# A spectral filter and a gated feed-forward on one core: the excursions of transform stage A moved off stage B, a third input buffer, an output buffer moved to a lasting pool, and the last copies moved to VectorE

## The chip, the cores and the metric

The kernel runs on one core of one Trainium2 chip. Times are device microseconds (us). A profiled run also leaves a trace of every instruction and DMA, with a span a little shorter than the timed run (925.2 us for 927.0). In its lines PE is TensorE, PEld its weight loads, DVE VectorE, ACT ScalarE, POOL GpSimd and SP SyncE; a q behind the name is the engine's queue of instructions, which also issues DMAs. The DMA share is the mean busy share of 16 DMA engines as the profile reports it, and it reads over 1 in places (1.31 from 68 to 70 us).

## The reference

```python
def _attn_ref(x, filt_r, filt_i):                  # x: (8, 3008, 256)
    X = np.fft.rfft(x, axis=1)                     # along the 3008 positions
    Y = X * (filt_r + 1j * filt_i)[None, :, :]     # filters: (1505, 256)
    return np.fft.irfft(Y, n=x.shape[1], axis=1)

def _moe_ref(x, w_gate, w_val, w_out):             # 24064 tokens, 256 -> 1536 -> 256
    gate = np.maximum(x @ w_gate, 0.0)
    val = x @ w_val
    return (gate * val) @ w_out
```

## The kernel before

The Fourier transform is done as matmuls. For each of 8 batches, stage A transforms along 94 positions and goes through DRAM (Abuf), stage B transforms along the other 32, multiplies by the filter, transforms back, and goes through DRAM (Dbuf), and stage C finishes the inverse and leaves yT, the input of the feed-forward. The feed-forward runs over 47 blocks of 512 tokens, 12 steps each, 564 steps in all. The work of the stages for later batches is laid into these steps, so that TensorE never has to run it alone.

From batch 2 on, stage A is "tiled". A chunk of x is loaded (`load_chunk`), GpSimd folds it with sums and differences (`fold_chunk`), and TensorE does 16 small fp32 products on 24 x 32 tiles of the array into four PSUM banks (`tiled_a`). The trace has 32 matmul records for them. I call this an excursion; each batch has four.

```python
pro = prologue.enter_context(tc.tile_pool(name="pro", bufs=1))      # closed before the main loop
...
def items_a(b):                                   # stage A of batches 0 and 1, in the prologue
    def one(c, j, st):
        if j == 0:
            st["asb"] = pro.tile([NROW, NC2 * D], BF16, tag="asb", bufs=4, name="asb")
        ...                                       # matmul into psA
        nc.scalar.copy(dst, psA[0:NROW])
        if j == 3:
            nc.sync.dma_start(..Abuf[b].., st["asb"])
...
def load_chunk(b, j):
    xp = XP[j % 2]                                # two chunk buffers
    ...                                           # 4 + 2 DMAs from SP, about 0.9 MB
def fold_chunk(b, j):
    t = fs.tile([128, 2, 512], FP32, tag="fold", bufs=2, name="fold")
    ...                                           # six tensor_tensor on GpSimd
def tiled_a(b, j):
    banks = [ps.tile([128, 2, D], FP32, tag=t, name="psF") for t in ("psv", "psg", "fft", "fft")]
    ...                                           # 16 matmuls, 4 copies to asf, 4 DMAs to Abuf
...
def gv(blk, ft, prods):                           # one step of the feed-forward
    ...                                           # 4 matmuls of 512 columns: psV, psG
    vsb = fs.tile([128, W], BF16, tag="vsb", bufs=3)
    nc.scalar.copy(vsb, psV[:, :W])
    nc.vector.scalar_tensor_tensor(prod, in0=psG[:, :W], scalar=0.0, in1=vsb, op0=ALU.max, op1=ALU.mult)
...
prologue.close()
fs = ctx.enter_context(tc.tile_pool(name="fs", bufs=2))   # takes over the prologue's memory
...
    end = (b * S // W - 1) * NFT + C_AT[0] - 5
    sb0 = 19 if b == 1 else end - 30 | 1          # first step of stage B of batch b
    ...
        for j in range(4):
            e = sb0 - 16 - NFT * (3 - j)          # excursions at sb0 -52, -40, -28, -16
            at_step(e - 23, lambda b=b, j=j: load_chunk(b, j))
            at_step(e - 22, lambda b=b, j=j: fold_chunk(b, j))
            at_step(e, lambda b=b, j=j: tiled_a(b, j))
    for i, f in enumerate(items_b(b)):
        at_step(sb0 + 2 * i, f)                   # stage B on steps sb0 to sb0 + 26
    at_step(sb0 + 27, lambda b=b: load_d(b))      # dC <- Dbuf, for stage C
```

## Time and profile before

| | before |
|---|---|
| time, median of 3 runs | 926.65 us (926.38 to 926.66) |
| span of the profiled run | 925.2 us |
| start of the first main-loop step | 61.2 us |
| last step's start to the end | 12.6 us |
| TensorE busy | 897.4 us |

The shortest way in is the chain of work that ended last, followed back from the end: its shares of the span by engine.

```profile
PE 90%; DMA 4%; ACT 2%; DVE 2%; issue 1%; SPq 0%; POOL 0%; ACTq 0%; POOLq 0%
```

TensorE (PE) carries 90% of it. What is not PE there is time in which TensorE, the engine that sets the pace, waits for someone else, and that is where a change of schedule can gain. A "step" in this text runs from its first load of a value weight (WvT) to the next step's; the steps' lengths are read off the trace.

### The profile page before, as it was taken

What the parts mean: (1) busy time and instruction counts of PE and PEld (TensorE: products, weight loads), DVE (VectorE), ACT (ScalarE), POOL (GpSimd) and SP (SyncE); (2) the same over time, 40 slices, a digit from 0 to 9 for tenths busy, and PEclk for the clock granted to TensorE, in tenths of its full rate; (3) what the DMA queues carried; (4) which work ended last, traced back from release to release, by engine and by line L of the source; (5) the groups of instructions that cost most, each with busy time, mean ns of one, the idle gap of its engine ahead of it and who ended that gap; (6) DMA issues with size and microseconds to landing.
All of it is one profiled execution on the core that took longest, in us unless ns stands there. A gap on an engine that the chain in (4) does not pass through costs nothing.

```text
span 925.2 us, 17992 instructions
## 1 busy us (share of the span) xinstructions
PE 897.4 (97%) x6488; PEld 546.7 (59%) x6602; DVE 576.8 (62%) x871; ACT 505.3 (55%) x897; POOL 260.6 (28%) x180
## 2 busy tenths in 40 slices
PE   8779999999999999999999999999999999999997
PEld 3435665566655665556655566655665566666665
DVE  3716865568655686557755577555875568655552
ACT  4655555555555555555555555555555555555553
POOL 4320444404444054322543125440444400000000
PEclk9899999999999999999999999999999999999999
DMA  9996345353453533553344533535335252231111
GB/s 253 257 249 131 104 129 146 89 128 104 126 150 88 128 104 116 155 118 86 108 146 137 114 105 111 153 100 124 99 120 170 64 118 64 63 102 36 35 30 50
DMA packets 106138, 109.04 MB, mean 118 GB/s; under 512 B 9794, under 2 KB 87362, under 8 KB 105410
## 3 DMA queue, kind: packets, MB, share of 16 engines
q1 hardware_dynamic: 101222, 103.77, 40.4%
q0 software_dynamic: 4512, 3.90, 2.7%
q8 instruction: 52, 0.85, 0.4%
q14 instruction: 36, 0.29, 0.1%
q10 hardware_dynamic: 316, 0.22, 0.1%
HBM read 61.94 MB, written 49.81 MB: 121 GB/s over the span
## 4 chain that ended last, share of the span: by engine, by line
PE 90%; DMA 4%; ACT 2%; DVE 2%; issue 1%; SPq 0%; POOL 0%; ACTq 0%; POOLq 0%
PE psG L444 26%; PE psO L463 25%; PE psV L444 24%; PE psF L321 4%; PE psA L275 3%; PE psD L383 2%; PE psD L382 2%; PE psX L363 2%; PE psY L428 2%; DVE prod L449 2%; ACT vsb L447 1%; DMA XF<-in_x_dram 1%; DMA Dbuf<-dsb 1%; DMA Abuf<-asb 1%; DMA out_dram<-osb 1%
## 5 line engine op out<-in xcount | busy, mean ns | idle before, releaser
L449 DVE SCALAR_TENSOR_TENSOR prod<-psG,vsb 128x512 bf16<-128x512 f32 x564 | 389.9, 692 | 288.5 <-ACT vsb L447 277.8
L447 ACT CAST vsb<-psV 128x512 bf16<-128x512 f32 x564 | 331.5, 588 | 270.2 <-PE psV L444 159.4
L463 PE MATMUL psO<-WoT,prod 128*128 128x256 bf16 x2256 | 336.6, 273 | 1.3
L444 PE MATMUL psG<-yT,WgT 128*128 128x512 bf16 x1102 | 331.1, 380 | 4.0
L444 PE MATMUL psV<-yT,WvT 128*128 128x512 bf16 x1041 | 318.7, 381 | 6.8 <-ACT vsb L447 4.5
L463 PEld LDWEIGHTS <-prod 128*128 128x128 bf16 x2256 | 220.6, 98 | 143.5
L444 PEld LDWEIGHTS <-WgT 128*128 128x128 bf16 x1128 | 110.3, 98 | 134.8 <-issue 2.2
L307 POOL TENSOR_TENSOR fold<-XP 128x1024 f32<-128x1024 f32 x24 | 56.4, 2348 | 416.0 <-DMA out_dram<-osb 151.4
L444 PEld LDWEIGHTS <-WvT 128*128 128x128 bf16 x1128 | 102.5, 98 | 38.5 <-issue 26.8
L385 ACT CAST dsb<-psD 128x512 bf16<-128x512 f32 x96 | 55.9, 587 | 51.8 <-PE psD L383 50.1
L468 ACT COPY osb<-psO 128x512 f32<-128x512 f32 (+1 forms) x96 | 55.3, 577 | 31.9 <-PE psO L463 24.5
L366 DVE TENSOR_TENSOR tt<-psX,Ftr 128x512 bf16<-128x512 f32 x96 | 65.2, 681 | 4.3 <-PE psX L363 4.3
L372 DVE TENSOR_TENSOR uu<-psX,Fti 128x512 bf16<-128x512 f32 x90 | 61.3, 681 | 0.0
L308 POOL TENSOR_TENSOR XP<-XP 128x1024 f32<-128x1024 f32 x24 | 56.4, 2350 | 1.9
L383 PE MATMUL psD<-uu,I2u 128*128 128x256 bf16 x192 | 47.7, 276 | 0.6 <-POOL uu L370 0.6
L382 PE MATMUL psD<-tt,I2t 128*128 128x256 bf16 x192 | 47.9, 276 | 0.0
L327 DVE CAST asf<-psF 128x512 bf16<-128x512 f32 x48 | 31.5, 687 | 16.6 <-PE psF L321 15.9
L363 PE MATMUL psX<-at,F 128*128 128x256 bf16 x192 | 37.8, 281 | 4.1 <-DMA at<-Abuf 4.1
L433 ACT CAST yT<-psY 128x512 bf16<-128x512 f32 x47 | 27.5, 585 | 24.0 <-PE psY L428 23.9
L435 DVE CAST yT<-psY 128x512 bf16<-128x512 f32 x47 | 32.0, 681 | 12.9 <-PE psY L428 12.9
L428 PE MATMUL psY<-M,dC 96*128 96x94 bf16 (+18 forms) x604 | 37.7, 199 | 1.1 <-DMA dC<-Dbuf 1.1
L321 PE MATMUL psF<-XP,WF 24*32 24x512 f32 x384 | 37.1, 597 | 0.0
(63 smaller groups left out, 437.9 us busy)
## 6 DMA issues: line engine op xcount, KB each, us to landing
dC<-Dbuf SPq DMA_DIRECT2D x64, 192.0 KB
XP<-in_x_dram SPq DMA_DIRECT2D x48, 256.0 KB
Dbuf<-dsb SPq DMA_DIRECT2D x31, 384.0 KB
XP<-in_x_dram SPq DMA_DIRECT2D x96, 96.0 KB
Abuf<-asf SPq DMA_DIRECT2D x96, 96.0 KB
at<-Abuf SPq DMA_DIRECT2D x48, 192.0 KB
out_dram<-osb SPq DMA_DIRECT2D x70, 94.0 KB
XF<-in_x_dram SPq DMA_DIRECT2D x12, 256.0 KB
```

The lines of the kernel that those rows point to most:

```text
L307: tt(t, xp[:, 0:2], xp[:, 2:4], op=ALU.add)
L308: tt(xp[:, 2:4], xp[:, 0:2], xp[:, 2:4], op=ALU.subtract)
L321: nc.tensor.matmul(banks[q][32 * c:32 * c + 32], WF[r:r + 24, c, :], fold[b, j][c][r:r + 24], start=True, stop=True, tile_position=(r, 32 ...
L363: nc.tensor.matmul(psX[:, i], F2[:, g + i, :], at[:, g + i, :], start=True, stop=True)
L366: nc.vector.tensor_tensor(tt, psX, Ftr[:, g:g + 2, :], op=ALU.mult)
L372: nc.vector.tensor_tensor(uu, psX, Fti[:, g:g + 2, :], op=ALU.mult)
L382: nc.tensor.matmul(psD[:, i], I2t[:, g + i, :], tt[:, i], start=True, stop=False)
L383: nc.tensor.matmul(psD[:, i], I2u[:, g + i, :], uu[:, i], start=False, stop=True)
L444: nc.tensor.matmul(pt[:, :W], w[:, h, ft * 128:(ft + 1) * 128], yt[:, h, :], start=(h == 0), stop=(h == 1))
L447: nc.scalar.copy(vsb, psV[:, :W])
L449: nc.vector.scalar_tensor_tensor(prod, in0=psG[:, :W], scalar=0.0, in1=vsb, op0=ALU.max, op1=ALU.mult)
L463: nc.tensor.matmul(psO[:, t % 2], prods[ft][:, t * 128:(t + 1) * 128], WoT[:, ft, :], start=(ft == 0), stop=(ft == NFT - 1))
```

## The change

Its intent is to let each excursion run in a step that has nothing but feed-forward work, to give x chunks the buffer that this spacing needs, to keep the output buffer of stage A out of the memory that the main loop takes over, and to free ScalarE at the end.

```diff
@@ items_a
-                st["asb"] = pro.tile([NROW, NC2 * D], BF16, tag="asb", bufs=4, name="asb")
+                st["asb"] = sb.tile([128, NC2 * D], BF16, tag="asb", bufs=4, name="asb")
@@ load_chunk, fold_chunk
-        xp = XP[j % 2]
+        xp = XP[(4 * b + j) % 3]
@@ tiled_a
-        asf = fs.tile([128, 2, 4, D], BF16, tag="asf", bufs=2, name="asf")
+        asf = sb.tile([128, NC2 * D], BF16, tag="asb", bufs=4, name="asb")
+        asf = asf.rearrange("p (n q d) -> p n q d", n=2, d=D)
@@ o_part
-            nc.scalar.copy(osb[:, t0 % 2:t % 2 + 1], psO[:, t0 % 2:t % 2 + 1])
+            copy = nc.vector.tensor_copy if last else nc.scalar.copy
+            copy(osb[:, t0 % 2:t % 2 + 1], psO[:, t0 % 2:t % 2 + 1])
@@ clear_chunks
-        for i in range(2):
+        for i in range(3):
@@ the schedule
-            for j in range(4):
-                e = sb0 - 16 - NFT * (3 - j)
-                at_step(e - 23, lambda b=b, j=j: load_chunk(b, j))
-                at_step(e - 22, lambda b=b, j=j: fold_chunk(b, j))
-                at_step(e, lambda b=b, j=j: tiled_a(b, j))
-            at_step(e + 4, lambda b=b: load_at_tiled(b))
+            for j, (l, e) in enumerate(((-66, -41), (-60, -33), (-54, -27), (-40, -17))):
+                at_step(sb0 + l, lambda b=b, j=j: load_chunk(b, j))
+                at_step(sb0 + l + 1, lambda b=b, j=j: fold_chunk(b, j))
+                at_step(sb0 + e, lambda b=b, j=j: tiled_a(b, j))
+            at_step(sb0 + e + 4, lambda b=b: load_at_tiled(b))
```

The slices that fit the larger buffer are left out. Line numbers shift by one or two: L444 (gv) is L445 after, L447 (vsb) L448, L468 (osb) L470, L476 (stores) L478, L428 (stage C) L429.

More of the change, by code (lines that the diff above doesn't have):

```diff
@@ L276, in one @@
                              start=True, stop=True)
-            dst = st["asb"][:, j * 512:(j + 1) * 512]
+            dst = st["asb"][:NROW, j * 512:(j + 1) * 512]
             nc.scalar.copy(dst, psA[0:NROW])
@@ L280, in one @@
                 nc.sync.dma_start(_ap(Abuf[b], c * NROW * NC2 * D, [[NC2 * D, NROW], [1, NC2 * D]]),
-                                  st["asb"])
+                                  st["asb"][:NROW])
         for c in range(N2 // NC2):
@@ L302, in fold_chunk @@
     def fold_chunk(b, j):
-        xp = XP[j % 2]
+        xp = XP[(4 * b + j) % 3]
         t = fs.tile([128, 2, 512], FP32, tag="fold", bufs=2, name="fold")
```

## The prediction

> **What bounds the kernel now.** I read the page's busy table first, then TensorE's waits, then the timeline around each place where TensorE is late, and last the clock in those stretches. In the page a line of the table is engine, busy us, share of the span, instructions:
>
> ```profile
> PE 897.4 (97%) x6488; PEld 546.7 (59%) x6602; DVE 576.8 (62%) x871; ACT 505.3 (55%) x897; POOL 260.6 (28%) x180
> ```
>
> TensorE is the bound: VectorE and ScalarE rest over a third of the span. 97% cannot be taken at its word, since a matmul is shown with its pipeline time (0.38 us for one whose successor starts 0.21 us later), so small gaps hide in it. I therefore measured steps. The main loop has 564 steps (47 blocks of 12), and I call a step the time from its first load of value weights to the next step's. 345 steps that do only feed-forward work have a median of 1.300 us (eight matmuls of 512 or 256 columns); 64 steps with a full share of stage B 1.955; 18 steps with one tiled A excursion 2.757; 6 with both, 4.288. Only what makes a step longer than its matmuls need can be won, so I looked for those. TensorE's waits (us in total, times, longest):
>
> ```profile
> PE psV L444 <- ACT vsb L447: 4.5, 1, 4.5
> PE psX L363 <- DMA at<-Abuf: 4.1, 1, 4.1
> ...
> PE psY L428 <- DMA dC<-Dbuf: 1.1, 1, 1.1
> ```
>
> The first stands at the start of the main loop. The view of the tile asb (A's output buffer) says whom it holds up:
>
> ```profile
> L280 SPq DMA_DIRECT2D Abuf<-asb x8: 303/309/437, 12.4 to 61.5; - x8
> ...
> POOL XP L562: 10.5, 1
> ACT vsb L447: 5.8, 1
> ```
>
> The last write of asb to DRAM is issued at 61.5; the first vsb copy, which reads only PSUM, waits for it, because vsb lies in memory that the closing prologue pool gives up and asb is in that pool. The completion counts put its landing at 67.33. The stretches (us, then busy us of PE, PEld, DVE, ACT, POOL; granted clock; DMA share; GB/s) show the second half of the price:
>
> ```profile
> 62.00:64.00 2.00, 1.83 (x7) 0.78 (x8) 0.07 (x1) 0.00 (x0) 0.00 (x0) 1.00 1.09 310
> 64.00:68.00 4.00, 0.00 (x0) 0.00 (x0) 0.00 (x0) 0.22 (x1) 0.31 (x1) 0.75 1.22 274
> 68.00:70.00 2.00, 1.58 (x4) 0.56 (x4) 1.29 (x2) 1.39 (x3) 2.00 (x2) 0.50 1.31 215
> 70.00:72.00 2.00, 2.00 (x6) 0.76 (x5) 0.69 (x1) 0.64 (x2) 1.24 (x1) 0.50 1.30 215
> 72.00:74.00 2.00, 2.00 (x8) 0.79 (x7) 1.19 (x2) 0.80 (x2) 0.00 (x0) 0.80 1.17 325
> ```
>
> No matmul for 4 us, then half clock until about 73. The other place is the excursion that falls on a stage B step. From the timeline (start, us, engine, line, instruction, count, idle before and who ended it), one such excursion, then one on a free step:
>
> ```profile
> 127.14 0.61 PE L321 MATMUL psF<-XP,WF 24*32 24x512 f32 x1
> ...
> 127.88 0.10 PEld L321 LDWEIGHTS psF<-XP,WF 24*32 24x32 f32 x1 [0.57 <-ACT dsb L385]
> ...
> 128.28 0.10 PEld L321 LDWEIGHTS psF<-XP,WF 24*32 24x32 f32 x1 [0.24 <-DVE uu L372]
> ...
> 129.50 0.38 PE L444 MATMUL psV<-yT,WvT 128*128 128x512 bf16 x1 [0.16 <-issue]
> ```
>
> ```profile
> 146.37 0.61 PE L321 MATMUL psF<-XP,WF 24*32 24x512 f32 x1
> ...
> 147.63 0.61 PE L444 MATMUL psV<-yT,WvT 128*128 128x512 bf16 x2
> ```
>
> 2.36 us against 1.26 for the same 32 matmuls: of the four PSUM banks that an excursion needs, two are the pair tagged "fft", which stage B's dsb copy and uu product still hold.
>
> [...] Here the last asb write, issued from SP, took 5.8 us (61.5 to 67.3), at a DMA share over 1. [...]
>
> **The change part by part.** (1) asb in the lasting pool. The built program agrees: the first vsb copy no longer waits for any asb write, only for things done by 61 (x loads, the small "last" read, the last A matmul). Saved: step 2 takes 6.114 us against 0.862 for its neighbour, 5.25; steps 3 and 4, at the low clock, 1.707 and 1.577, 0.85 and 0.71 too much. Sum **6.8 us**, all on TensorE's path. The wait for yT before step 0 (0.69 in the timeline) stays.
>
> (2) Excursions moved. With a batch's stage B on steps 0 to 26 after sb0 and a period of 72, the first of each batch's four sat at -52, which is +20 of the batch before. The new places, -41, -33, -27, -17, are +31 and later: all free, and none shares a step with stage C. Batches 2 to 7 have one bad one each: 6 x ((4.288 - 1.955) - (2.757 - 1.300)) = 6 x 0.876 = **5.3 us**. The step after is 1.207 in both kinds, so nothing is paid later. The other 18 move from one free step to another: 0. They leave step 5 of a block, where the output copy uses ScalarE, for 4, 0 and 6; adding up the copies (0.59 and 0.69 us each) after an excursion at step 4, every bank is free before TensorE wants it.
>
> (3) A third chunk buffer: 1.8 us more memset on GpSimd (3.54 for two) near 61 to 67, beside everything; the first chunk load is at step 27 now. It allows the close spacing. The fold tile keeps two buffers, so the third fold waits for the first excursion: six operations, 2 x 2.35 + 4 x 1.27 = 9.8 us, due 14 steps later (14 x 1.30 + 1.36 = 19.6). Hidden.
>
> (4) Last copies on VectorE. The last matmul ends at 919.4 (913.58 + 5.84), the last copy starts at 921.73, because ScalarE also issues stores, and its issues wait:
>
> ```profile
> 917.49 2.87 ACTq L476 DMA_DIRECT2D out_dram<-osb  x3
> 920.47 0.37 ACT L468 COPY osb<-psO 128x256 f32<-128x256 f32 x1 [3.01 <-DMA out_dram<-osb]
> ...
> 921.73 0.37 ACT L468 COPY osb<-psO 128x256 f32<-128x256 f32 x1 [0.89 <-ACT osb L468]
> ```
>
> The copies will come 2 us earlier, but three issues in 2.87 us against two in 0.70 shows that the stores wait for the landing of stores before them, on a semaphore used again. That stays. I choose **0.5 us** of the 2.3.
>
> Sum: 6.8 + 5.3 + 0.5 = 12.6; 926.65 - 12.6 = **914.1 us**, 1.4% less.
>
> **The rivals.** First, a new wait takes the old one's place. The loop start comes 6.8 us earlier for loads whose issue does not move. Landing in this trace and new need: second half of gate weights 65.3, step 6 at 67.6; third dC part 69.3, step 8's stage C at 69.8; second half of output weights 73.4, about 76. The middle one has 0.5 us; a DMA share over 1 speaks for trouble, the unchanged queue order against it. It would cost 0.5 to 2 us, more if the clock drops again. Second, the dC wait: one stage C start out of six waited (1.1 us near 483), another had only about 0.3 us to spare. The x loads around it move; the two outcomes, no wait and two or three, are -1 to +2 us. Third, excursions at the new places find their own bank or copy waits; 24 x 0.2 would be 5 us and take back part 2. Against it: the 18 free ones agree within 0.15 us. Fourth, the end is bound by stores and part 4 is nil: +0.5; or the semaphores clear early: -1.5.
>
> **Range and chances.** All parts right and the dC wait gone gives 912; part 4 nil with two new waits of 1.5 us gives 917.5. I take 911.8 to 917.6. Faster by over 2% needs below 908.1, which is 6 us beyond every gain I can find: 2%. Slower by 2% needs 19 us of new waiting: 1%.
>
> **What would show it.** TensorE's waits no longer name vsb; clock 1.00 through 62 to 76; the first main-loop steps all near 0.86; no step above 2.8 us among those with an excursion; idle before weight loads in excursions ended by nothing of stage B; last output copies on VectorE within 1 us of their matmuls, and the end about 4 to 5 us after the last matmul. It is wrong if psY waits for dC near 70, if the excursions at the new steps exceed 2.757, or if a fold of GpSimd ends a wait of TensorE.

## The result, and the profile after

The changed kernel took 913.28 us (913.1 to 913.37, 4 runs) against 926.65 in the same rounds (926.38 to 926.96). A ratio in this document is the mean time of one kernel's runs over that of the other's runs of the same rounds, so it is not quite the ratio of the medians. Here it is 0.9855 (95% interval 0.9838 to 0.9872), 13.4 us less.

The chain of the changed kernel shows the gain in one line: what was DMA, ACT, DVE and "issue" has become PE.

```profile
PE 95%; DMA 3%; SPq 0%; ACT 0%; POOL 0%; DVE 0%; issue 0%; ACTq 0%; POOLq 0%
```

TensorE's waits after the change (us in total, times, longest) no longer name vsb in the first place, nor psY waiting for dC at all. What is left are the start-up waits and sub-microsecond ones (the longest four):

```profile
PE psX L364 <- DMA at<-Abuf: 3.9, 1, 3.9
PE psJ L489 <- DVE junk L495: 2.5, 1, 2.5
PE psA L275 <- DMA XF<-in_x_dram: 1.7, 2, 1.5
PE psV L445 <- ACT yT L434: 0.7, 1, 0.7
```

The same stretches at the start of the main loop (us, busy us of PE, PEld, DVE, ACT, POOL, then granted clock, DMA share, GB/s): TensorE is busy and the clock stays at 1.00, while the DMA columns are almost those of before.

```profile
64.00:68.00 4.00, 4.00 (x21) 1.82 (x19) 3.30 (x5) 2.63 (x5) 2.16 (x2) 1.00 1.21 281
68.00:70.00 2.00, 2.00 (x16) 1.06 (x15) 1.55 (x3) 1.45 (x3) 0.00 (x0) 1.00 1.31 214
70.00:72.00 2.00, 2.00 (x17) 1.01 (x15) 1.38 (x2) 1.69 (x4) 0.00 (x0) 1.00 1.30 217
```

The first excursion of batch 2 in the timeline, now on a free step: first product at 135.90, next feed-forward matmul at 137.16, that is 1.26 us where the kernel before needed 2.36.

```profile
135.90 0.61 PE L321 MATMUL psF<-XP,WF 24*32 24x512 f32 x1
...
137.16 0.60 PE L445 MATMUL psV<-yT,WvT 128*128 128x512 bf16 x2
```

Where the 13.96 us between the two profiled spans come from:

| stretch | before, us | after, us | difference |
|---|---|---|---|
| to the first step's start | 61.16 | 61.03 | -0.12 |
| steps 0 to 11 | 18.29 | 11.48 | -6.81 |
| steps 12 to 562 | 833.16 | 826.40 | -6.77 |
| last step's start to the end | 12.63 | 12.37 | -0.26 |

The third row splits further. The six excursions on stage B steps gave 6 x 0.876 = 5.26. Step 272 had been 2.848 us against a median of 1.609 for its kind, because stage C waited for dC: 1.24. The remaining 0.27 is mostly a handful of excursions a little under the median of 2.757.

### The profile page after: what moved, and what is told of

It reads as the page before. It is cut to its first block, busy times and chain, and to the rows that moved or that the text cites. A ratio compares the mean times of both kernels' runs of the same rounds, so it can differ in the third digit from the quotient of the medians.

```text
span 911.3 us, 18044 instructions
## 1 busy us (share of the span) xinstructions
PE 896.0 (98%) x6602; PEld 545.7 (60%) x6602; DVE 578.0 (63%) x875; ACT 500.8 (55%) x893; POOL 262.4 (29%) x181
## 4 chain that ended last, share of the span: by engine, by line
PE 95%; DMA 3%; SPq 0%; ACT 0%; POOL 0%; DVE 0%; issue 0%; ACTq 0%; POOLq 0%
PE psV L445 27%; PE psG L445 27%; PE psO L464 26%; PE psF L321 3%; PE psA L275 3%; PE psY L429 2%; PE psD L383 2%; PE psD L384 2%; PE psX L364 2%; DMA XF<-in_x_dram 1%; DMA Abuf<-asb 1%; DMA at<-Abuf 0%; DMA out_dram<-osb 0%; SPq L178 0%; SPq L478 0%
## 5 line engine op out<-in xcount | busy, mean ns | idle before, releaser
L448 ACT CAST vsb<-psV 128x512 bf16<-128x512 f32 x564 | 332.0, 589 | 244.7 <-PE psV L445 206.4
L445 PE MATMUL psV<-yT,WvT 128*128 128x512 bf16 x1128 | 335.9, 379 | 0.9 <-ACT yT L434 0.7
L445 PE MATMUL psG<-yT,WgT 128*128 128x512 bf16 x1128 | 335.3, 379 | 0.0
L445 PEld LDWEIGHTS <-WgT 128*128 128x128 bf16 x1128 | 110.0, 98 | 133.8 <-issue 0.5
L445 PEld LDWEIGHTS <-WvT 128*128 128x128 bf16 x1128 | 102.3, 98 | 33.1 <-issue 20.9
L470 ACT COPY osb<-psO 128x512 f32<-128x512 f32 x92 | 53.9, 586 | 22.7 <-PE psO L464 20.3
L328 ACT CAST asb<-psF 128x512 bf16<-128x512 f32 x48 | 25.8, 589 | 32.5 <-PE psF L321 32.5
L328 DVE CAST asb<-psF 128x512 bf16<-128x512 f32 x48 | 30.9, 686 | 17.3 <-PE psF L321 14.5
L429 PE MATMUL psY<-M,dC 96*128 96x94 bf16 (+18 forms) x604 | 37.5, 198 | 0.0
```

What stands on the lines that cost most here:

```text
L328: copy(asf[:, :, q, :], banks[q])
L445: nc.tensor.matmul(pt[:, :W], w[:, h, ft * 128:(ft + 1) * 128], yt[:, h, :], start=(h == 0), stop=(h == 1))
```

## The experiments

Twelve runs were made, all correct. The first three are parts of the change taken alone.

**Only the buffer** (e1_pool).

```diff
 # from the kernel before
-                st["asb"] = pro.tile([NROW, NC2 * D], BF16, tag="asb", bufs=4, name="asb")
+                st["asb"] = sb.tile([NROW, NC2 * D], BF16, tag="asb", bufs=4, name="asb")
```

> The kernel before with only A's output buffers of the prologue moved to the lasting pool. Theory (the wait of the first vsb copy on the last A store, plus the half clock after it): 6.8 us less than before, about 919.8 us; steps 2, 3 and 4 of the main loop at 0.86 us, clock 1.00 from 62 to 76. Rival (another load takes the wait's place): 1 to 5 us less, with a new TensorE wait near 65 to 76. The excursions on stage B steps stay at 4.29 us, and the wait for dC near 480 may stay or move.

Measured: 919.70 us against 926.70, ratio 0.9928 (0.9915 to 0.9941), 6.7 us less. Steps 2, 3 and 4 take 0.863, 0.864 and 0.863 us, steps 0 to 11 together 11.48 (the changed kernel: 11.48), the six excursions on stage B steps still 4.288. The theory holds, and no later load took over the wait, so the rival is out. Stage C did not wait for dC in this profile, although no load was moved; I come back to this below.

**Only the steps and the third buffer** (e2_steps): the schedule, `XP` and `clear_chunks` parts of the diff above, applied to the kernel before.

> The kernel before with only the excursions moved and the third chunk buffer. Theory: 5.3 us from the six bad excursions, and 1.2 us from the wait for dC, which I now take to be an effect of where the x chunks are loaded and not of chance: 6.5 us less in all, about 920.2 us; all 24 steps with an excursion at 2.65 to 2.9 us, the first dC part landing 2 to 4 us ahead of its use for every batch (before: -1.4 to 2.3 us). Rival (the dC wait was chance): 5.3 us less, and the room before dC's use as in the kernel before. The stall at step 2 stays at 6.1 us.

Measured: 920.59 us, ratio 0.9936 (0.9924 to 0.9947), 5.9 us less. In its profile steps 12 to 562 take 826.68 us, 6.5 less than before, as worked out. Its first step began 1.0 us later (62.19), but its steps 0 to 11 took 17.29 us against 18.29, so the profiled span is 6.5 less too, and the 5.9 of the timed runs differs from 6.5 by less than the interval. Over all the profiles the first step starts between 60.9 and 62.3 us whatever the edit; in this run 0.7 us of it is stage C waiting for batch 0's dC at 61.2, and what decides the rest stays open. No excursion is over 2.92 us. This run leaves `asf` in its old pool, and its steps 12 to 562 are within 0.3 us of the changed kernel's 826.40, so moving `asf` is worth no more than that.

**Only the copies** (e3_copy): the `o_part` part of the diff, applied to the kernel before.

> The kernel before with only the last block's output copies on VectorE. Theory (stores wait for the landing of earlier stores on the same semaphore): 0.2 to 0.4 us less, although the last copy starts about 2.3 us earlier. Rival (the copies set the end): 2 us less.

Measured: 926.77 us, ratio 1.0 (0.9988 to 1.0012). The timed runs cannot resolve a quarter of a microsecond. The profile can: from the last step's start to the end 12.39 us against 12.63, so 0.24 less. The rival's 2 us are excluded.

The three parts alone add up to 12.6 us by their ratios, the whole gave 13.4. The difference is within the intervals.

**The stall without the loss of clock** (e4_warm). The kernel before, with matmuls that nobody reads laid into the stall.

```diff
 # from the kernel before
     at_step(2, clear_chunks)
+    def fill(n):
+        psJ = ps.tile([128, 512], FP32, tag=fft_tag(), name="psJ")
+        for i in range(n):
+            nc.tensor.matmul(psJ, WvT[:, 0, 0:128], yTs[0][:, 0, :], start=True, stop=True)
+    at_step(1, lambda: fill(20))
```

> The kernel before with 20 matmuls of 512 columns added, results unused, queued behind step 1 so that they fill most of the 4.5 us stall at step 2 (20 x 0.216 = 4.3 us). It parts the stall from the clock. Theory (an idle TensorE loses its clock): step 2 stays near 6.1 us, steps 3 and 4 fall from 1.71 and 1.58 to 0.86 us, 1.5 us less than before in all, clock 1.00 from 64 to 74. Rival (steps 3 and 4 are slow because ScalarE and VectorE catch up): they stay at 1.6 to 1.7 us and the time stays at 926.6 us.

Measured: 924.18 us, ratio 0.9972 (0.9959 to 0.9985). The same stretches in its profile, with ScalarE and VectorE idle from 64 to 68 as before but the clock at 1.00:

```profile
64.00:68.00 4.00, 4.00 (x20) 1.85 (x19) 0.00 (x0) 0.12 (x1) 0.21 (x1) 1.00 1.21 273
68.00:70.00 2.00, 1.85 (x9) 0.68 (x8) 1.35 (x3) 1.54 (x3) 2.00 (x2) 1.00 1.30 214
```

The added matmuls stand in step 1, which takes 5.18 us, and step 2 then takes 1.34, so the expected 6.1 of step 2 is to be looked for there. Steps 3 and 4 take 0.861 and 0.864 us instead of 1.707 and 1.577, so they had been slow through the clock (0.50 from 68 to 72 us in the kernel before, 1.00 here) and not through copies that had to catch up. Steps 0 to 11 take 16.24 us against 18.29: of the 6.8 us, 2.05 are the clock and 4.76 the wait, as far as one profile of each can tell. The clock's part is larger than the 1.56 of steps 3 and 4, since step 2's own matmuls, from 68.4 on, had run at half clock too (0.50 from 66.0 to 72.8). The price of the stall is not fixed: in four profiles that have it without the added matmuls, steps 0 to 11 take 17.29 (e2_steps), 18.29 (before), 18.40 (e3_copy) and 18.88 us (e8_bank). The half clock lasted 3.4 us in the first of these and 6.8 in the others, and it began 2.1 (before) to 4.0 us (e2_steps) after the last matmul. The rest of this run's gain lies in the loop, where no wait for dC occurred.

**Was the wait for dC chance?** In the prediction I treated it as such. The traces let one measure the room: from the landing of the first dC part of a batch (by its completion counts; two parts for batch 6) to its first use in stage C.

| room, us | batch 2 | 3 | 4 | 5 | 6 |
|---|---|---|---|---|---|
| before | 0.2 | 1.5 | -1.4 | 1.0 | 0.8 |
| buffer only (e1_pool) | 1.3 | 0.8 | 0.7 | 0.5 | 0.9 |
| copies only (e3_copy) | -0.2 | 1.3 | -0.9 | 0.9 | 0.7 |
| steps and buffer (e2_steps) | 1.8 | 2.9 | 3.4 | 2.6 | 3.9 |
| after | 2.4 | 2.7 | 3.2 | 3.0 | 3.9 |
| after, once more | 1.6 | 3.0 | 3.4 | 3.4 | 3.8 |
| third load at +21 (e6_load21) | 1.4 | 0.6 | 0.9 | 0.5 | 0.9 |

Batch 7 is left out; its first part has over 2 us in all of them. So with the old places the room is near zero and chance decides who waits; the new places give about 2 us more. Among one profile of each kernel, three of the five with the old places wait for dC within the loop (before, e3_copy, e8_bank), and none of the eight with the new ones. The test moves one load back to where one had been:

```diff
 # from the changed kernel
-... in enumerate(((-66, -41), (-60, -33), (-54, -27), (-40, -17))):
+... in enumerate(((-66, -41), (-60, -33), (-51, -27), (-40, -17))):
```

> The changed kernel with one number changed: each batch's third x chunk is loaded at step +21 of the batch before (where the kernel before had a load), not at +18. Theory (the load sits ahead of the last D store in the queue and on the DMA engines): the first dC part lands 1 to 3 us later, the room before its use falls from 2.4-3.9 us to 0-2 us, at most one wait of up to 1 us, time 0 to 1 us more than the changed kernel. Rival (the wait for dC was chance): the room stays at 2.4 us or more.

> The changed kernel once more, unedited, as the measure for the three beside it. 13.4 us less than before, ratio 0.9855; end 12.4 us after the start of the last step; first dC part landing 2.4 us or more ahead of its use.

Measured: 914.19 us (ratio 0.9875) against 913.67 for the changed kernel on the same chip (0.9868). The room falls as the theory says, to 0.5 to 1.4 us, and no wait results; the difference in time is within the noise. So the effect of the load on the room is shown, and that the waits follow from the room is supported by the count above only. The repeat of the changed kernel gained 12.2 us in the medians where 13.4 was expected, and its room in batch 2 was 1.6 us where 2.4 or more was; its end, 12.41, was as expected. SP's own queue around batch 4, in the timeline (start, us, line, what, count), shows the mechanism. The kernel before:

```profile
464.89 1.58 SPq L294 DMA_DIRECT2D XP<-in_x_dram  x4
466.52 1.17 SPq L298 DMA_DIRECT2D XP<-in_x_dram  x2
...
473.04 0.48 SPq L387 DMA_DIRECT2D Dbuf<-dsb  x1
480.49 5.01 SPq L406 DMA_DIRECT2D dC<-Dbuf  x8
```

The changed kernel, in the same view:

```profile
448.30 1.16 SPq L298 DMA_DIRECT2D XP<-in_x_dram  x2
...
460.99 0.35 SPq L388 DMA_DIRECT2D Dbuf<-dsb  x1
465.91 3.99 SPq L407 DMA_DIRECT2D dC<-Dbuf  x8
```

The experiment, in the same view:

```profile
455.51 1.16 SPq L298 DMA_DIRECT2D XP<-in_x_dram  x2
...
462.06 0.35 SPq L388 DMA_DIRECT2D Dbuf<-dsb  x1
468.91 3.98 SPq L407 DMA_DIRECT2D dC<-Dbuf  x8
```

The reader compares the start of the last D store with that of the first dC load, which waits for the store's landing: 7.5 us in the kernel before with an x load issued 5 to 8 us ahead of it, 4.9 us in the changed one with the load over 11 us ahead, 6.9 us with the load put back to 5 to 10 us ahead. The completion counts show what the D store stands behind. In the kernel before, the last part of the x load lands at 476.4, five output stores issued behind it between 476.6 and 479.6, and the D store at 480.5. In the changed kernel the last part of the x load has landed at 456.8, before the D store is issued.

**Which banks make an excursion long** (e8_bank). The kernel before with one word changed:

```diff
 # from the kernel before
-... for t in ("psv", "psg", "fft", "fft")]
+... for t in ("psv", "psg", "pso", "fft")]
```

> The kernel before with one bank of each excursion taken from the output product's pair instead of the second of the fft pair. Theory (the excursions on stage B steps are long because two of their banks are the fft pair that stage B holds): these six steps fall from 4.29 us to 3.7 to 4.0, 2 to 3.5 us less than before in all; the 18 on free steps stay at 2.76. Rival (they are long because of the order of work and the drain of the array): they stay at 4.29 and the time within 0.5 us.

Measured: 922.39 us, ratio 0.9957 (0.9945 to 0.9969), 4.0 us less, more than expected. The six on stage B steps fall from 4.288 to 3.890 us: one of the two waits for stage B is left. In the timeline of weight loads the one for dsb stays, and the one of 0.24 us for uu, which the prediction showed, is gone:

```profile
128.97 0.10 PEld L321 LDWEIGHTS psF<-XP,WF 24*32 24x32 f32 x1 [0.54 <-ACT dsb L385]
```

The theory holds for these. But the 18 on free steps fell as well, from 2.758 to 2.649 us on average, which neither theory had foreseen: with two banks of one pair an excursion took 0.11 us longer even on steps without stage B. Why is open.

**Is the third chunk buffer needed?** (e5_two_chunks). With two buffers and the loads left at -54 and -40 the kernel did not build: the build reported a deadlock, since the third load would take the first chunk's buffer ahead of its excursion. So the loads come as soon as the buffers are free:

```diff
 # from the changed kernel
-        xp = XP[(4 * b + j) % 3]
+        xp = XP[j % 2]
-        for i in range(3):
+        for i in range(2):
-... in enumerate(((-66, -41), (-60, -33), (-54, -27), (-40, -17))):
+... in enumerate(((-66, -41), (-60, -33), (-40, -27), (-32, -17))):
```

> The changed kernel with two chunk buffers again, the excursions where they are now, and the third and fourth chunk loaded as soon as their buffer is free (-40 and -32). Worked out from before: a load takes about 7 us (5 steps) and a fold 9.8 us (7.5 steps), 12.5 of the 13 steps from -40 to the third excursion at -27, and 15 steps from -32 to the fourth. Theory (the third buffer is what makes the close spacing possible): the third excursion waits for the fold, 0 to 2 us in each of six batches, 0 to 10 us slower than the changed kernel, with TensorE's waits naming a POOL fold. Rival (two buffers were enough with these loads): the same time as the changed kernel within 1 us and no such wait.

Measured: 986.72 us, ratio 1.0651 (1.0637 to 1.0666). The direction was right, the size not: some 12 us per batch in place of 0 to 2. TensorE's waits in this run (us in total, times, longest) are headed by GpSimd's fold:

```profile
PE psF L321 <- POOL XP L309: 32.8, 6, 6.5
```

The weight load that waited in batch 3, from the timeline (start, us, engine, line, what, count, idle before and who ended it):

```profile
283.13 0.17 PEld L321 LDWEIGHTS psF<-XP,WF 24*32 24x32 f32 x2 [6.22 <-POOL XP L309]
```

My 7 us for a load was wrong. In this trace the third chunk of batch 3 is issued from 265.2 on, and its last part lands at 276.8, 11.5 us later; the fold ends at 287.1, and no weights had been loaded since 276.9 (283.13 - 6.22). The mean clock falls to 0.96 (0.995 in the changed kernel), and in the stretches of this stall to 0.76 (276 to 288 us) and 0.62 (288 to 294). In the changed kernel such a load takes as long (202.2 to 213.4), with time to spare; over the 48 chunks of the kernels before and after, none lands in less than 10.0 us. In both places the two 256 KB parts land last; their semaphore is counted up five times each, that of a store of 128 rows 16 times. Why they land late was not shown.

**What holds the end** (e7_cut, e9_cutq, e10_actcopy). The copies on VectorE start within 0.9 us of what they wait for, yet the end hardly moved. In the changed kernel's timeline:

```profile
899.88 5.84 PE L464 MATMUL psO<-WoT,prod 128*128 128x256 bf16 x52
...
902.29 6.16 ACTq L478 DMA_DIRECT2D out_dram<-osb  x9
...
905.76 0.42 DVE L470 COPY osb<-psO 128x256 f32<-128x256 f32 x1 [0.89 <-DMA out_dram<-osb]
```

Matmuls end at 905.7 and the last copy at 906.2, but ScalarE's nine stores stretch from 902.3 to 908.4. The stores use eight semaphores in turn, and each waits for the landing of the store that used its semaphore last: the store of 94 rows issued at 901.49 lands at 905.23, and the next store with its semaphore starts at 905.25. The first eight include the uncut stores of 94, 18, 76 and 52 rows of the block before last, and stores whose data were ready at 903.6 start only after 905.2. So those stores were cut into a part with a multiple of 16 rows and a rest, as the stores of the last block already are. By the completion counts of the changed kernel (three for a store of 94 rows, 16 for one of 90, 13 for one of 72) a store of 94 rows takes a median 4.9 us from the start of its issue to the last count and never under 3.5, one of 90 or 72 rows a median 2.1; the 4.0, 3.2 and 1.7 in the expectation of e7_cut are not found again by this count. That the number of rows has to be a multiple of 16 was not shown: no run tests another.

```diff
 # e7_cut, from the changed kernel
-                    cut = w // 16 * 16 if last else 0
+                    cut = w // 16 * 16 if last or blk == NB - 2 and s == 11 else 0
 # e9_cutq, in addition
-                            eng = nc.scalar if last and (t + i) % 2 else nc.sync
+                            eng = nc.scalar if (t + i) % 2 and last or c0 and not last else nc.sync
 # e10_actcopy, from e9_cutq
-            copy = nc.vector.tensor_copy if last else nc.scalar.copy
+            copy = nc.scalar.copy
```

> The changed kernel with the last five stores of the block before last cut, as the last block's are, into a part with a multiple of 16 rows and a rest (nine stores). The stores of 94, 18 and 76 rows are the ones whose landing the last block's stores wait for; in the main loop a store of 94 rows lands a median 4.0 us after its issue and never under 3.2, one of 90 or 72 rows a median 1.7. [...] Theory (that landing holds up the end): the end comes 0.7 to 1.5 us earlier, last step's start to end 11 to 11.7 us instead of 12.4. Rival (the rate of issue sets the end): four more issues of about 0.35 us on SP, no gain or up to 0.5 us worse.

> As the run before it, and the rests are issued from ScalarE, which is idle then. Theory (landing of the uncut stores): about the same gain as with the cut alone, 1 to 2 us. If only this one gains, SP's rate of issue was the limit of the cut alone.

> The kernel with cut stores and rests issued from ScalarE, with the last copies back on ScalarE. Alone, the copies on VectorE were worth 0 to 0.3 us, hidden by stores that waited. Theory (with the stores freed the copies count): last step's start to end 11.5 to 13 us instead of 10.8, 1 to 2 us slower than the same kernel with VectorE copies. Rival: the same within 0.3 us.

| | time, us | ratio to before | last step's start to the end, us |
|---|---|---|---|
| changed kernel, same chip as the next two | 913.67 | 0.9868 | 12.41 |
| e7_cut | 913.82 | 0.9868 | 12.07 |
| e9_cutq | 912.47 | 0.9851 | 10.81 |
| e10_actcopy (another chip) | 913.44 | 0.9863 | 11.58 |

The cut alone frees the semaphores (in its trace the stores of both queues follow each other at 0.3 to 0.6 us after 904), but SP then has 17 stores to issue and is the limit: both the theory and its rival are half right. With the rests issued from ScalarE the end comes 1.6 us earlier in the profile and about 1.2 us in the medians. With that, the place of the copies seems to matter: 0.8 us in the profile, where it had been worth 0.25. The timed runs do not show it. Each median lies 13.4 us under that of the kernel before on its own chip (926.81 - 913.44 and 925.83 - 912.47), the intervals of the ratios overlap, and one of the four runs of e10_actcopy, at 916.0, raises its ratio.

**All of it together** (e11_best).

```diff
 # from e9_cutq
-... for t in ("psv", "psg", "fft", "fft")]
+... for t in ("psv", "psg", "pso", "fft")]
-... in enumerate(((-66, -41), (-60, -33), (-54, -27), (-40, -17))):
+... in enumerate(((-66, -40), (-60, -33), (-54, -28), (-39, -16))):
```

> The changed kernel with what the runs showed to gain: the cut stores with rests issued from ScalarE, one bank of each excursion from the output product's pair, and three of the four excursions one step over (-40, -28, -16, fourth load -39) so that they follow the output copy of step 5. Worked out from the runs: excursions on free steps 2.65 us instead of 2.75, 24 x 0.1 = 2.4 us; stores 1.5 us; 3.9 us less than the changed kernel, ratio to before 0.981 to 0.983, about 909.5 to 910.5 us. Against it: the excursion at step 0 of a block takes the output product's other bank and the product at step 6 must wait for its copy; up to 1 us in each of six batches.

Measured: 910.91 us (910.17 to 911.18), ratio 0.9833 (0.982 to 0.9847), the lowest of all, though just short of the expected 0.981 to 0.983 and with an interval that overlaps that of e9_cutq. The 24 excursions take 63.26 us together against 65.93 in the changed kernel, 2.67 less. The feared wait at step 6 did not come. But its end took 12.34 us in the profile, so the stores' gain of e9_cutq was not kept there: with the same edit, one issue from SP took 1.5 us (900.3 to 901.8) and those behind it started late; the first store of the end took 3.5 us to land (899.0 to 902.5), where in e9_cutq it took 1.4. I did not settle why; the gain at the end is therefore not to be relied upon to more than its 0 to 1.6 us.

## Why the prediction was right

*The bound.* TensorE carried the chain before and does so more after (90%, then 95%). Right.

*Part 1, the wait on the last store of asb and the lost clock: 6.8 us.* Measured 6.81 in the profile and 6.7 with this part alone (e1_pool, 5.5 to 7.9 by its interval). That 6.81 agrees to the digit is no proof of skill: the forecast was read off the same profile of the kernel before, and other profiles of the stall would have given 5.8 to 7.4. The split was off: 5.25 and 1.56 were given for the stall and the clock, e4_warm shows 4.76 and 2.05. The sum does not depend on it. The reading of the clock was rough as well: the 0.75 of 64 to 68 is 2 us at full and 2 us at half clock, the fall coming 2.1 us after the last matmul (63.9 to 66.0), and the full clock returned at 72.8, 4.4 us after matmuls went on at 68.4.

*Part 2, the excursions: 5.3 us.* 5.26 in the profile, from the same steps as the forecast, and 5.9 with the third buffer in e2_steps (4.9 to 7.0 by its interval), which includes the dC wait below. All 24 are between 2.665 and 2.896 us in the changed kernel. "Nothing is paid later" held: the step after is 1.207 in both kernels. That the bad ones were long through the shared banks is supported by e8_bank, which took one shared bank away and 0.4 us with it.

*Part 3, the third buffer: hidden.* Right, and needed: without it the same places, with the loads as early as two buffers allow, cost 74 us more than the changed kernel, by the ratios 1.0651 and 0.9855.

*Part 4, the copies: 0.5 of 2.3 us.* The mechanism (stores wait for stores) was right; the term is 0.25 us. The term was over-sized: the last copy ends at 906.2, but stores still wait for earlier ones, and the last is issued at 908.8. e9_cutq, which frees them, gains 1.6 us in the profile with the same copies.

*The rivals.* The first did not come about: the third dC part landed at 69.1 us, and step 8 did not wait. The second is where the prediction failed in a step: it took the dC wait near 483 as able to go either way, "-1 to +2 us", and left it out of the sum. It went away (1.24 us in the profile), and the likely reason could have been read from the schedule: an x load no longer stands shortly ahead of D's last store. e6_load21 puts it there again and takes the room away, though no wait came back. In the profile this missing term, less the 0.24 us that the copies fell short, accounts for more than the difference between 12.6 and 13.4; how often the timed runs of the kernel before have that wait is not known. So the sum came out near in part because an over-sized and a missing term stood against each other. The third rival, waits of the moved excursions, did not come about. The fourth, stores that bind the end, did.

*The signs.* All but two were seen: no vsb among TensorE's waits, clock 1.00 from 62 to 76, steps 1 to 7 at 0.86, copies within 1 us of their matmuls, no fold ending a wait of TensorE. The two were too sharp: "no step above 2.8 us" (the longest excursion step is 2.896), and the end "4 to 5 us after the last matmul" (905.7 to 911.3 is 5.6). Taken by the letter, one sign of being wrong was seen too, excursions over 2.757 us: several take 2.758 and one 2.896. Two margins were misreckoned: 908.1 is 6 us under the sum's 914.1 and only some 3 under all gains named together (about 911), and 2% slower would have needed some 31 us of new waiting, not 19, since 12.6 are gained first.

## What to carry to other kernels

Here a buffer that was still being stored when its pool closed held up the first copy into the memory it gave up, though that copy never touches the store: ScalarE stood idle for 5.80 us before it, and moving the buffer gained 6.7 us (e1_pool). Give buffers that outlive a phase to a pool that does too. Price a stall of TensorE at more than its length where the granted clock falls with it, here to 0.50: 4.76 us of waiting cost 6.8, and the same stall cost between 5.8 and 7.4 from one profile to the next. And when a wait in the trace is a matter of tenths, measure the room of all its siblings before calling it chance, because here moving one large load in the queue shifted the room of all five batches, from 1.6 to 3.9 us down to 0.5 to 1.4 (e6_load21).
